# A finished expert's output copies moved into the code between experts

## The chip, the cores and the metric

One Trainium2 chip, one core of it. The metric is device time in microseconds (us) of one execution; the median of three runs of the kernel before is 878.82 us (875.96 to 879.72). Engines are named as in the profile: PE multiplies matrices (PEld loads its weights), ACT, DVE and POOL work on rows of data, SP issues DMAs. PSUM is the memory that PE writes to, SBUF the memory that the others work in.

## The reference, cut to what matters

Three stages follow one another. An attention stage with 4 batches, 8 heads, 512 local and 32 global tokens gives a matrix `x` of 2176 tokens by 512. A mixture of 8 experts then sends each token to one expert:

```python
logits = x @ w_gate
expert_idx = np.argmax(logits, axis=1)
for e in range(E):                      # 8 experts
    mask = expert_idx == e
    xe = x[mask]
    h = np.maximum(xe @ w1[e], 0.0)     # 512 -> 1024
    out[mask] = gate_w[mask, None] * (h @ w2[e])   # 1024 -> 512
```

A last feed-forward stage computes `(h - tanh(h)) @ w_out` with `h = x @ w_in` (512 to 2048 to 512). How many tokens an expert gets is known only while the kernel runs. Products are formed from a high and a low part of each operand, in three matmuls, to keep float32 accuracy.

## The kernel before

The attention stage scatters each token's row to its expert's list in DRAM (`xs`). The experts are then worked through in eight places, 0 to 7; which expert stands at which place is chosen by how many tokens each has. At a place the code is this:

- `put_ids` (L1228) copies the token numbers of the place's rows to `ids`.
- `place(e)` (L1195) is a tree of comparisons on the place's token count. It ends in one of several arms, written out one after the other in the program: one for each width from the place's largest down to 256 in steps of 32, and one for 128. Each engine compares and jumps for itself.
- Each arm is a whole expert at a fixed width N. `expert` (L1105) goes through eight blocks m of 128 hidden units: first layer into `pL1` (L1010), ReLU and split into high and low by ACT (L1013) and DVE (L1014), second layer into the four PSUM banks `pL2` (L1021), two blocks behind. `expert_small` (L1126) is the arm for 128 tokens, with operands exchanged; its result is in the bank `pL2[0]`, is added up in SBUF (L1181) and transposed by PE back into `pL2[0]` (L1183).
- Both arms end with the outputs: copies from PSUM to the tiles `yst` (`emit_Y`, L1026, two on ACT and two on DVE at width N; L1185 in the small arm, one on each) and four DMAs from `yst` to the output matrix `yc` in DRAM (L1027, L1192), at a column that is known only at run time.
- After the tree all arms meet again. `emit_XT` (L995) brings in the next place's rows: for each of four k, PE transposes the tiles of `xrow` into a PSUM bank (L999), ACT casts the bank into the high part `xT[0]` (L1001) and DVE subtracts it from the bank into the low part `xT[1]` (L1002). The banks are `pX[0]`, `pX[1]`, `pL1[1]` and again `pX[0]`, so that the fourth transposes wait for DVE's first subtraction. `load_x` (L987) then has SP fetch the rows of the place after next.

Beside this, all through the arms, the experts' weights arrive by DMA in `raw` buffers (L120, L122), six blocks ahead, and ACT, DVE and POOL split them into high and low (`split_from`, L928 to L937); in some blocks DVE and ACT also convert the last stage's weights (`conv_bits`, L942). Just before its outputs an arm splits two blocks of the next expert's weights (`ahead` and `split`).

`hint(e + 1)` (L1212) is a small tree of comparisons in each arm, after block 2 (after the first pair of blocks but one in the small arm). Its leaf marks the next place's arm, and puts a prefetch instruction for that branch on each engine. In the last place the branch marked is `over` (L1285), which is taken when an expert has more than 512 tokens.

The last arm of place 7 also starts the last stage: `split_y0`, and `emit_H(0)` (L1053) ahead of its own outputs.

The order is written out by hand; engines run their own queues in order and wait for each other by semaphores.

Of the kernel before, what the change touches and what calls it, by code (L numbers as in the profile page):

```python
# [46 lines left out]
def body(ctx: ExitStack, tc: tile.TileContext, q_l, k_l, v_l, q_g, k_g, v_g,  # L47
         w_gate, w1, w2, w_in, w_out, out):
    nc = tc.nc
# [7 lines left out]
    KD = DM // 128  # L57
# [10 lines left out]
    idf = const.tile([128, 128], F32, name="idf")  # L68
# [36 lines left out]
    yc = [dram.tile([128, T + CAP], F32, name=f"yc{k}") for k in range(KD)]  # L105
# [18 lines left out]
    def load_raw(c):  # L124
        if c < NC:
            load_w(raw[c % NR], eids[c // MF], c % MF)
# [57 lines left out]
    for kind in ("first", "mid", "last"):  # L184
        m = attc.tile([128, W], F32, name=f"mask_{kind}")
# [135 lines left out]
    for j in range(4):  # L321
# [6 lines left out]
                          in_=tokid[:, 0:NXB * NB])  # L328
# [392 lines left out]
    for n in range(lo, NT0):  # L721
# [4 lines left out]
        if n == lo:  # L726
# [8 lines left out]
            for j in range(B):  # L735
                nc.sync.dma_start(out=vg[:, j].rearrange("g (h d) -> g h d", h=H),
                                  in_=v_g[j].rearrange("h g d -> g h d"))
# [86 lines left out]
    for w in LAST.split():  # L824
        t, m = w.split(".")
# [88 lines left out]
    pX = [psL.tile([128, 512], F32, name=f"pX_{j}") for j in range(2)]  # L914
    pL2 = [psL.tile([128, 512], F32, name=f"pL2_{j}") for j in range(4)]
# [6 lines left out]
    yst = [mc.tile([128, 512], F32, name=f"yst{j}") for j in range(4)]  # L922

    def split(c, eng=None):
        if c < NC:
            split_from(raw[c % NR].bitcast(F32), c % NS, eng)
# [60 lines left out]
    def load_x(e, step=2):  # L987
        if e >= E:
            return
        v = xsr[bass.ds(xos[e], CAP), :].rearrange("(j p) w -> p j w", p=128)  # L990
        for j in range(0, tiles(e), step):
            r = slice(j, min(j + step, tiles(e)))
            nc.sync.dma_start(out=xrow[:, r], in_=v[:, r])
# [10 lines left out]
    def emit_L1(s, m, N, first=False):  # L1004
        ps = pL1[m % 2]

        for c in (slice(0, 256), slice(N - 256, N)) if first and N > 256 else (slice(0, N),):
            for a, x in ((0, 0), (1, 0), (0, 1)):
                for k in range(KD):
                    nc.tensor.matmul(ps[:, c], w1s[s][a][:, k], xT[x][:, k, c], start=a + x + k == 0,  # L1010
                                     stop=x == 1 and k == KD - 1)
        h = hT[m % 3]
        nc.scalar.activation(out=h[0][:, 0:N], in_=ps[:, 0:N], func=ACTF.Relu)  # L1013
        nc.vector.scalar_tensor_tensor(out=h[1][:, 0:N], in0=ps[:, 0:N], scalar=0.0, in1=h[0][:, 0:N].bitcast(F32),  # L1014
                                       op0=ALU.max, op1=ALU.subtract)

    def emit_L2(s, m, N):
        h = hT[m % 3]
        for j in range(KD):
            for a, x, st, sp in ((0, 0, m == 0, False), (0, 1, False, False), (1, 0, False, m == MF - 1)):  # L1020
                nc.tensor.matmul(pL2[j][:, 0:N], w2s[s][a][:, 128 * j:128 * (j + 1)], h[x][:, 0:N], start=st, stop=sp)  # L1021

    def emit_Y(N, yo):
        for j in range(KD):
            copy = nc.vector.tensor_copy if j % 2 else nc.scalar.copy
            copy(out=yst[j][:, 0:N], in_=pL2[j][:, 0:N])  # L1026
            nc.sync.dma_start(out=yc[j][:, bass.ds(yo, N)], in_=yst[j][:, 0:N])  # L1027
# [11 lines left out]
    while t0 < T:  # L1039
        n = min(NB2, T - t0)  # L1040
# [20 lines left out]
    def load_wout():  # L1061
        for m in range(PW, PW + NO):
            wout_load(m)
# [12 lines left out]
    def tiles(p):  # L1076
        return -(-sizes(p)[0] // 128)


    def sizes(p):  # L1080
        most = T // (RANKS[p - 1] + 1) if p else T
        most = min(CAP, 32 * -(-most // 32))
        return tuple(range(most, 255, -32)) + (128,)
# [18 lines left out]
        if (e, m) in convs:  # L1102
            pre_conv1(convs[e, m], tmp64)

    def expert(e, N, yo):  # L1105
        for m in range(MF):
            c = e * MF + m
            emit_L1(c % NS, m, N, c == 0)
            if m > 1:
                emit_L2((c - 2) % NS, m - 2, N)  # L1110
            ahead(e, m)
            if m == 2:
                hint(e + 1)
        split((e + 1) * MF + LS)
        load_raw((e + 1) * MF + LS + NR)
        if e == E - 1:
            split_y0()
            load_wout()
        for m in range(MF - 2, MF):
            emit_L2((e * MF + m) % NS, m, N)  # L1120
        if e == E - 1:
            emit_H(0)
        emit_Y(N, yo)


    def expert_small(e, yo):  # L1126
        NQ = MF // 2

        def L1(q, ks):
            s = (e * MF + 2 * q) % NS  # L1130
            ps = pL1[q % 2][:, 0:256]
            for k in ks:
                for a, x, st, sp in ((0, 0, k == 0, False), (0, 1, False, False), (1, 0, False, k == KD - 1)):
                    nc.tensor.matmul(ps, xT[x][:, k, 0:128], w1a[a][:, s:s + 2, k, :], start=st, stop=sp)
            if q > 0 and KD - 1 in ks:
                nc.scalar.activation(out=hs[q % 2], in_=ps, func=ACTF.Relu)
            elif len(ks) == KD:
                nc.vector.tensor_scalar(out=hs[q % 2], in0=ps, scalar1=0.0, scalar2=None, op0=ALU.max)

        def TH(q):  # L1140
            pt = pX[q % 2][:, 0:256]
            for i in range(2):
                nc.tensor.transpose(pt[:, 128 * i:128 * (i + 1)], hs[q % 2][:, 128 * i:128 * (i + 1)], idf)
            t = hT[q % 3]
            nc.scalar.copy(out=t[0][:, 0:256], in_=pt)
            nc.vector.tensor_tensor(out=t[1][:, 0:256], in0=pt, in1=t[0][:, 0:256].bitcast(F32), op=ALU.subtract)


        def L2(q, c=slice(0, DM), ps=pL2[0]):
            last = NQ - 1  # L1150
            for i in range(2):
                m = 2 * q + i
                s = (e * MF + m) % NS
                for a, x, st, sp in ((0, 0, q in (0, last) and i == 0, False), (0, 1, False, False),
                                     (1, 0, False, q in (last - 1, last) and i == 1)):
                    nc.tensor.matmul(ps[:, c], hT[q % 3][x][:, 128 * i:128 * (i + 1)], w2s[s][a][:, c],
                                     start=st, stop=sp)

        for q in range(NQ):
            first = (KD, 2, 1, 1)[q]  # L1160
            L1(q, range(first))
            if q > 0:
                TH(q - 1)
            if q or e == 0:
                split(e * MF + 2 * q + LS, nc.vector)
            L1(q, range(first, KD))
            if q > 0:
                L2(q - 1)
            ahead(e, 2 * q, None, True)
            if q < NQ - 1:  # L1170
                ahead(e, 2 * q + 1, nc.vector, True)
            if q == 1:
                hint(e + 1)
        if e == E - 1:
            split_y0()
            load_wout()
        TH(NQ - 1)
        nc.scalar.copy(out=yst[3], in_=pL2[0])
        for c, ps in ((slice(0, 256), pX[0]), (slice(256, 512), pL1[0])):
            L2(NQ - 1, c, ps)  # L1180
            nc.vector.tensor_tensor(out=yst[2][:, c], in0=ps[:, c], in1=yst[3][:, c], op=ALU.add)  # L1181
        for k in range(KD):
            nc.tensor.transpose(pL2[0][:, 128 * k:128 * (k + 1)], yst[2][:, 128 * k:128 * (k + 1)], idf)  # L1183
        for c, copy in ((slice(0, 256), nc.scalar.copy), (slice(256, 512), nc.vector.tensor_copy)):
            copy(out=yst[3][:, c], in_=pL2[0][:, c])  # L1185
        ahead(e, MF - 1, nc.vector, True)
        split((e + 1) * MF + LS)
        load_raw((e + 1) * MF + LS + NR)
        if e == E - 1:
            emit_H(0)  # L1190
        for k in range(KD):
            nc.sync.dma_start(out=yc[k][:, bass.ds(yo, 128)], in_=yst[3][:, 128 * k:128 * (k + 1)])  # L1192


    def place(e, i=0):  # L1195
# [8 lines left out]

    def arm(e, n):
        if n == 128:
            expert_small(e, yos[e])
        else:
            expert(e, n, yos[e])


    def hint(e, lo=0, hi=None):  # L1212
# [15 lines left out]
    def put_ids(xr, yo):  # L1228
        nc.sync.dma_start(out=ids[bass.ds(yo, CAP), :], in_=xsr[bass.ds(xr, CAP), DM:DM + 1])
# [10 lines left out]
    for c in range(LS):  # L1240
        split(c)
        if c + NR < MF:
            load_raw(c + NR)
    banks = pX + pL2
    cnts = values(0, 0, mybir.ALL_ENGINES, T)
    hint(0)
    for j in range(4):
# [10 lines left out]
    yos = values(2, 0, SP, T) + values(2, 1, SP, T)  # L1258
    cnts += values(0, 1, mybir.ALL_ENGINES, T)
    for e in range(E):  # L1260
        put_ids(xos[e], yos[e])
        if e == E - 1:
            mxc = nc.values_load(offi[0:1, 3, 0:1], min_val=0, max_val=T)
            with tc.If(mxc <= CAP):
                load_y0()
        place(e)
        if e + 1 < E:
            emit_XT(range(KD), (pX[0], pX[1], pL1[1], pX[0]), tiles(e + 1))
            load_x(e + 2)


    def block_over(e, xb, j, yo):
# [148 lines left out]
    for c in range(NCH + LO):  # L1421
# [10 lines left out]
        if wo_hl:  # L1432
            m = wo_hl.pop(0)
            conv_hl(tmpo[m % 2], wo[m][0], wo[m][1], nc.gpsimd)
        emit_v(c)
        if wo_next[0] < M2 and 4 * (c - WL) >= 5 * (wo_next[0] - PW):
            m = wo_next[0]
# [40 lines left out]
```

## Time and profile before

| | us |
|---|---|
| median of three runs (875.96 to 879.72) | 878.82 |
| the profiled execution | 877.86 |
| its span, first to last instruction | 876.1 |
| PE busy | 797.0 |
| DVE busy | 668.2 |
| ACT busy | 484.2 |
| POOL busy | 324.9 |

The mean granted clock of PE in that execution is 0.974 of full speed. The profile's page gives busy time by engine, the span in forty slices, the DMA queues, the chain of work that ended last, and the costliest groups of instructions. Behind it stand views of the same trace: the timeline (instructions in order of time), sums by stretches, the waits and the records of single lines. Times in them are microseconds from the start of the span. In this execution the places ran with widths 480, 512, 128, 320, 128, 288, 256 and 256; the experts take from 188 to 476 us, the last stage from there to the end.

### The profile page before, as it was taken

The page shows a single profiled execution, that of the slowest core. Times are in us where ns is not written, and L with a number is a line of the kernel's source. Part 1 is how long each engine was busy: PE and PEld are TensorE (multiplying, and loading weights), DVE is VectorE, ACT ScalarE, POOL GpSimd, SP SyncE. Part 2 cuts the span into 40 slices and gives each one's busy share as a digit, 9 for nine tenths or more (in the row PEclk, how much of TensorE's full clock was granted, in tenths as well). Part 3 has the DMA queues.
Part 4 walks back from the last instruction along what each step waited for, and adds up shares of the span by engine and source line. Part 5 has one row for each costly group of instructions (what it writes and reads, how often), then busy time and mean ns, then how long its engine had stood idle before and what let it go on. Part 6 is the DMA issues. An engine that isn't in the chain of part 4 may idle for free. (4 is left out here: it accounts for less than half of the span.)

```text
span 876.1 us, 16545 instructions
## 1 busy us (share of the span) xinstructions
PE 797.0 (91%) x5456; PEld 694.6 (79%) x5456; DVE 668.2 (76%) x1428; ACT 484.2 (55%) x1177; POOL 324.9 (37%) x405
## 2 busy tenths in 40 slices
PE   8989999969899787796969988999999999999997
PEld 6767777758788687686969866799899999998885
DVE  6879999854568676775546999988788778778784
ACT  6777877533334343353524655565565566556564
POOL 8222352423213334342511565533433333343332
PEclk9999999979999899998979999999999999999999
DMA  6699964445846798889533223010000010010000
GB/s 146 148 266 228 271 175 139 135 146 151 251 144 205 185 217 246 213 199 297 164 70 101 65 107 108 1 46 28 13 34 28 1 46 19 1 43 1 13 25 24
DMA packets 145261, 102.96 MB, mean 118 GB/s; under 512 B 76608, under 2 KB 124224, under 8 KB 145088
## 3 DMA queue, kind: packets, MB, share of 16 engines
q1 hardware_dynamic: 142368, 92.08, 39.0%
q0 software_dynamic: 2720, 8.95, 2.7%
q8 instruction: 63, 1.03, 0.5%
q14 instruction: 110, 0.90, 0.4%
HBM read 78.75 MB, written 22.27 MB: 115 GB/s over the span
## 5 line engine op out<-in xcount | busy, mean ns | idle before, releaser
L1371 POOL TENSOR_TENSOR u<-u,z 128x384 f32<-128x384 f32 (+1 forms) x96 | 122.1, 1271 | 226.3 <-ACT u L1369 226.2
L936 POOL TENSOR_TENSOR w2s<-raw,w2s 128x512 fp32r<-128x512 f32 x64 | 90.8, 1427 | 199.7 <-ACT w2s L935 155.2
L1010 PE MATMUL pL<-xT,w1a 128*128 128x256 f32 (+4 forms) x588 | 109.6, 344 | 20.1 <-issue 8.5
L1010 PEld LDWEIGHTS pL<-xT,w1a 128*128 128x128 f32 x588 | 96.6, 210 | 29.7 <-issue 12.1
L1399 PE MATMUL pL<-wo,gT 128*128 128x512 f32 x417 | 108.9, 394 | 0.0
L1021 PE MATMUL pL<-hT,w2s 128*128 128x256 f32 (+4 forms) x576 | 98.6, 324 | 0.0
L1021 PEld LDWEIGHTS pL<-hT,w2s 128*128 128x128 f32 x576 | 87.7, 190 | 6.5
L1399 PEld LDWEIGHTS pL<-wo,gT 128*128 128x128 f32 x417 | 77.5, 188 | 14.3
L1386 DVE TENSOR_TENSOR gT<-g,gT 128x384 fp32r<-128x384 f32 (+1 forms) x64 | 79.1, 1236 | 0.7 <-ACT gT L1364 0.7
L365 ACT ACTIVATE P<-sc,mx 128x224 f32<-128x224 f32 x128 | 60.6, 477 | 12.0 <-DVE mx L356 11.4
L1376 DVE TENSOR_TENSOR g<-pL,z 128x384 f32<-128x384 f32 (+1 forms) x64 | 34.0, 531 | 42.9 <-ACT d L1359 42.9
L1053 PE MATMUL pL<-xT,wih 128*128 128x384 f32 x256 | 65.2, 335 | 1.5 <-DVEq L1285 1.5
L936 DVE TENSOR_TENSOR w1a<-raw,w1a 128x512 fp32r<-128x512 f32 x64 | 62.9, 986 | 4.1 <-ACT w1a L935 2.9
L1358 ACT ACTIVATE z<-pL 128x384 f32<-128x384 f32 (+1 forms) x64 | 30.2, 472 | 62.9 <-PE pL L1053 59.4
L1014 DVE SCALAR_TENSOR_TENSOR hT<-pL,hT 128x256 fp32r<-128x256 f32 (+4 forms) x48 | 25.0, 520 | 50.1 <-ACT hT L1013 42.7
L1053 PE MATMUL pL<-yB,wih 128*128 128x384 f32 (+1 forms) x256 | 59.5, 318 | 0.0
L1369 ACT ACTIVATE u<-z,c1t 128x384 f32<-128x384 f32 (+1 forms) x96 | 58.2, 606 | 0.0
L1370 ACT ACTIVATE mk<-z,nth 128x384 bf16<-128x384 f32 (+1 forms) x96 | 56.8, 592 | 0.0
L1382 DVE SCALAR_TENSOR_TENSOR g<-u,g 128x384 f32<-128x384 f32 (+1 forms) x96 | 55.0, 573 | 0.0
L1399 PE MATMUL pL<-wo,xT 128*128 128x512 f32 x207 | 54.4, 395 | 0.0
L1013 ACT ACTIVATE hT<-pL 128x256 fp32r<-128x256 f32 (+4 forms) x48 | 22.2, 463 | 52.3 <-PE pL L1010 52.3
L1053 PEld LDWEIGHTS pL<-xT,wih 128*128 128x128 f32 x256 | 46.7, 188 | 4.3 <-ACTq L1285 1.8
(294 smaller groups left out, 1889.3 us busy)
## 6 DMA issues: line engine op xcount, KB each, us to landing
raw<-in_moe_w_dram SPq DMA_DIRECT2D x128, 256.0 KB, 5.1
xs<-zrow SPq DMA_DIRECT2D x32, 258.0 KB, 4.8
raw<-in_moe_w_in_dram SPq DMA_DIRECT2D x16, 512.0 KB, 5.0
raw<-in_moe_w_out_dram SPq DMA_DIRECT2D x16, 512.0 KB, 3.6
xrow<-xs SPq DMA_DIRECT2D x12, 516.0 KB, 5.1
nk<-in_k_l_dram SPq DMA_DIRECT2D x32, 128.0 KB, 3.6
nq<-in_q_l_dram SPq DMA_DIRECT2D x32, 128.0 KB, 3.7
v<-in_v_l_dram SPq DMA_DIRECT2D x12, 256.0 KB, 4.5
```

Source lines behind the costliest of these rows:

```text
L365: nc.scalar.activation(out=P[:, j, 0:W], in_=sc[:, j], func=ACTF.Exp, scale=-1.0, bias=mx[:, j:j + 1], accum_out=sums[n][:, 2 * ip + j, h: ...
L936: (nc.gpsimd if lo else nc.vector).tensor_tensor(out=dl, in0=t[:, lo:lo + 512], in1=dh.bitcast(F32), op=ALU.subtract)
L1010: nc.tensor.matmul(ps[:, c], w1s[s][a][:, k], xT[x][:, k, c], start=a + x + k == 0, stop=x == 1 and k == KD - 1)
L1021: nc.tensor.matmul(pL2[j][:, 0:N], w2s[s][a][:, 128 * j:128 * (j + 1)], h[x][:, 0:N], start=st, stop=sp)
L1053: nc.tensor.matmul(ps[:, 0:n], a[:, m, k], y[x][:, k, 0:n], start=st, stop=sp)
L1369: nc.scalar.activation(out=u, in_=z, func=ACTF.Identity, scale=C2, bias=c1t)
L1370: nc.scalar.activation(out=mk, in_=z, func=ACTF.Relu, bias=nth)
L1371: nc.gpsimd.tensor_tensor(out=u, in0=u, in1=z, op=ALU.mult)
L1376: nc.vector.tensor_tensor(out=g, in0=h, in1=z, op=ALU.mult)
L1382: nc.vector.scalar_tensor_tensor(out=g, in0=u, scalar=C0, in1=g, op0=ALU.add, op1=ALU.mult)
L1386: nc.vector.tensor_tensor(out=t[1][:, 0:n], in0=g, in1=t[0][:, 0:n].bitcast(F32), op=ALU.subtract)
L1399: nc.tensor.matmul(p, g[a][:, 128 * j:128 * (j + 1)], w, start=st, stop=sp)
```

## The change

The copies and the output DMAs leave the arms. `emit_Y` is called once for each place, in the common code after the tree: behind `emit_XT` and `load_x`, so after the casts of the next place's rows. Its width is no longer the arm's N but the largest of the place: 512 at places 0, 1, 3, 5 and 7, 320 at place 2, 384 at place 4, 448 at place 6. The small arm's transposes write to the first 128 columns of four banks, so that `emit_Y` finds its outputs where it finds those of the other arms; its own two copies and four DMAs go. The first place's rows are transposed into `pL2` in place of `pX` and two banks of `pL2`. `hint` moves from block 2 to block 0 (in the small arm from the second pair to the first).

```diff
-    def expert(e, N, yo):
+    def expert(e, N):
...
             ahead(e, m)
-            if m == 2:
+            if m == 0:
                 hint(e + 1)
...
         if e == E - 1:
             emit_H(0)
-        emit_Y(N, yo)
-    def expert_small(e, yo):
+    def expert_small(e):
...
-            if q == 1:
+            if q == 0:
                 hint(e + 1)
...
         for k in range(KD):
-            nc.tensor.transpose(pL2[0][:, 128 * k:128 * (k + 1)], yst[2][:, 128 * k:128 * (k + 1)], idf)
-        for c, copy in ((slice(0, 256), nc.scalar.copy), (slice(256, 512), nc.vector.tensor_copy)):
-            copy(out=yst[3][:, c], in_=pL2[0][:, c])
+            nc.tensor.transpose(pL2[k][:, 0:128], yst[2][:, 128 * k:128 * (k + 1)], idf)
         ahead(e, MF - 1, nc.vector, True)
         split((e + 1) * MF + LS)
         load_raw((e + 1) * MF + LS + NR)
         if e == E - 1:
             emit_H(0)
-        for k in range(KD):
-            nc.sync.dma_start(out=yc[k][:, bass.ds(yo, 128)], in_=yst[3][:, 128 * k:128 * (k + 1)])
...
-    banks = pX + pL2
+    banks = pL2
...
         if e + 1 < E:
             emit_XT(range(KD), (pX[0], pX[1], pL1[1], pX[0]), tiles(e + 1))
             load_x(e + 2)
+
+        emit_Y(sizes(e)[0], yos[e])
```

## Rows read from the trace of the kernel before

**Rows 1.** Sums by stretch: length, busy time (count) per engine, clock, DMA share, GB/s.

```profile
181.00:478.00 297.00, 249.67 (x1478) 223.94 (x1479) 182.80 (x269) 120.47 (x246) 90.34 (x64) 0.93 0.68 189
478.00:862.00 384.00, 373.66 (x1923) 333.69 (x1922) 324.07 (x522) 232.01 (x520) 161.68 (x142) 1.00 0.10 33
```

**Rows 2.** Timeline, places 0 to 1: start, length, instruction, [idle before <-what ended it].

```profile
228.79 0.62 ACT L935 CAST w2s<-raw 128x512 fp32r<-128x512 f32 x1 [0.24 <-issue]
...
233.52 0.56 ACT L1026 COPY yst<-pL 128x480 f32<-128x480 f32 x1 [0.74 <-PE pL L1021]
...
234.76 1.10 PE L999 MATMUL pX<-idf,xrow 128*128 128x128 f32 x8 [0.62 <-issue]
...
236.20 1.07 ACT L1001 CAST xT<-pX 128x512 fp32r<-128x512 f32 x2 [2.12 <-PE pX L999]
...
237.63 1.29 DVE L1002 TENSOR_TENSOR xT<-pX,xT 128x512 fp32r<-128x512 f32 x2 [2.80 <-ACT xT L1001]
...
239.91 10.06 PE L1010 MATMUL pL<-xT,w1a 128*128 128x512 f32 x36 [0.81 <-ACT xT L1001]
```

**Rows 3.** Timeline, places 1 to 2.

```profile
282.49 0.62 ACT L935 CAST w2s<-raw 128x512 fp32r<-128x512 f32 x1
...
284.69 0.59 ACT L1026 COPY yst<-pL 128x512 f32<-128x512 f32 x1 [0.77 <-PE pL L1021]
...
285.70 0.85 PE L999 MATMUL pX<-idf,xrow 128*128 128x128 f32 x6 [0.37 <-issue]
...
289.38 0.86 ACT L1001 CAST xT<-pX 128x384 fp32r<-128x384 f32 x2 [4.10 <-issue]
...
290.60 1.02 DVE L1002 TENSOR_TENSOR xT<-pX,xT 128x384 fp32r<-128x384 f32 x2 [4.54 <-ACT xT L1001]
...
291.83 3.92 PE L1134 MATMUL pL<-w1a,xT 128*128 128x256 f32 x18
```

**Rows 4.** PE's jump records near 281 and 352 us: count, min/median/max ns, start.

```profile
L1200 PEldq COMPARE_BRANCH  x1: 4418/4418/4418, 281.1 to 281.1; - x1
...
L1200 PEldq COMPARE_BRANCH  x1: 2410/2410/2410, 351.9 to 351.9; - x1
```

**Rows 5.** Timeline, places 3 to 4.

```profile
350.23 0.88 PE L999 MATMUL pX<-idf,xrow 128*128 128x128 f32 x6 [1.46 <-issue]
...
354.58 2.38 PE L1134 MATMUL pL<-w1a,xT 128*128 128x256 f32 x18 [2.10 <-ACT w1a L935]
```

**Rows 6.** Sums by stretch around two boundaries; columns as in the first group.

```profile
240.70:244.10 3.40, 3.40 (x9) 2.63 (x8) 0.00 (x0) 0.00 (x0) 0.00 (x0) 0.50 0.61 183
244.10:250.00 5.90, 5.90 (x27) 4.88 (x26) 3.80 (x6) 2.23 (x4) 1.01 (x1) 1.00 0.01 1
348.00:355.00 7.00, 2.94 (x21) 2.23 (x20) 3.32 (x7) 2.77 (x6) 1.51 (x1) 1.00 0.87 277
```

**Rows 7.** Timeline, places 2 to 3, the small arm's end.

```profile
309.40 0.42 DVE L1181 TENSOR_TENSOR yst<-pL,yst 128x256 f32<-128x256 f32 x1 [0.23 <-PE pL L1156]
...
311.28 0.69 DVE L936 TENSOR_TENSOR w1a<-raw,w1a 128x512 fp32r<-128x512 f32 x1
```

**Rows 8.** Sums by stretch in place 3; columns as in the first group.

```profile
316.00:336.00 20.00, 16.32 (x112) 16.05 (x110) 11.33 (x17) 7.34 (x15) 5.58 (x4) 1.00 0.92 194
```

**Rows 9.** Timeline, place 3, PE's longest stop there and DVE ahead of it.

```profile
334.95 0.43 DVE L946 TENSOR_SCALAR tmp<-raw 128x512 int32<-128x512 int32 x1 [5.94 <-DMA raw<-in_moe_w_in_dram]
...
336.56 3.42 PE L1010 MATMUL pL<-xT,w1a 128*128 128x320 f32 x12 [4.24 <-DVE hT L1014]
```

**Rows 10.** PE's prefetch record in place 7, and the timeline behind it.

```profile
L1473 PEldq BRANCH_PREFETCH_HINT  x1: 41/41/41, 442.3 to 442.3; - x1
...
442.39 3.63 PE L1010 MATMUL pL<-xT,w1a 128*128 128x256 f32 x17 [3.74 <-issue]
450.60 4.42 PE L1010 MATMUL pL<-xT,w1a 128*128 128x256 f32 x19 [4.57 <-issue]
```

**Rows 11.** Waits of PE for nothing visible: us in total, times, longest.

```profile
PE pL L1010 <- issue: 8.5, 3, 4.6
```

More of the change, by code (lines that the diff above doesn't have):

```diff
@@ L1206, in arm @@
         if n == 128:
-            expert_small(e, yos[e])
+            expert_small(e)
         else:
-            expert(e, n, yos[e])
+            expert(e, n)
     def hint(e, lo=0, hi=None):
```

## The prediction

> **What bounds the kernel now.** Read the sums by stretch first [rows 1]. From 478 us on PE is busy 373.7 of 384 us, so whatever the experts save before that reaches the end. Between 181 and 478 us PE is busy 249.7 of 297 us at a granted clock of 0.93: some 47 us of idle time, and part of the busy time at the lower clock. The change acts on the boundaries between places, so the timeline there comes next.
>
> At places 0 to 1 [rows 2] ACT's last cast in the arm is at 228.79; it then waits for PE to finish the second layer, since its copies come last. The second copy starts at 233.52, and only behind it does ACT leave the arm. PE starts the next rows' transposes at 234.76, but ACT's first cast comes at 236.20 and DVE's first subtraction at 237.63, 0.84 us after that cast's result (two casts take 1.07, pipelined). DVE's subtraction lets PE make the fourth transposes, and the first layer starts at 239.91. At places 1 to 2 [rows 3] it is plainer: ACT's copy starts at 284.69, PE transposes at 285.70, and ACT's cast starts at 289.38 after 4.10 us idle "by issue", that is, waiting for nothing that the profile shows. The copies run up to the jump out of the arm, and from the jump to the common code ACT starts nothing for 2.7 us (233.52 to 236.20) and 4.7 us (284.69 to 289.38). [...]
>
> PE pays too, but earlier: its sequencer runs ahead of the array and jumps at 281.1 for 4.42 us [rows 4], while queued matmuls are still running, so only 0.37 us of idle time is left at 285.70 [rows 3].
>
> **The change part by part.** *Copies out of the arms, places 0 to 1.* The last work of ACT in the arm becomes the cast at 228.79, of DVE a subtraction at about the same time. ACT jumps 4.7 us sooner (233.52 less 228.79), more than the 2.7 us that the jump costs, and DVE likewise; both stand in the common code when PE's transposes arrive. Four transposes of the eight at 234.76 take about 0.6 us with their drain, so ACT's cast starts near 235.4, is done near 236.0, and DVE starts at 236.0 where it started at 237.63: 1.6 us. PE's fourth transposes, ACT's fourth cast and the first layer follow DVE at unchanged distances. Gain 1.6. What is late next is PE's walk through the comparisons, which sits inside the 0.81 us before 239.91 and moves with it.
>
> *Places 1 to 2.* ACT's jump moves from 284.7 to 282.5 [rows 3], so its 4.7 us end near 287.2 instead of 289.38: 2.2 us. But another wait takes over. At places 3 to 4 nothing of ACT is late, and still PE starts the small arm only at 354.58, because its jump into the arm at 351.9 takes 2.41 us [rows 4, 5]; that is 354.35, or 4.1 us after it entered the common code at 350.23. If the same 4.1 us hold from 285.70, PE can't start before 289.8, with the first matmul near 290.1, against 291.83. Gain 1.7; without that bound 2.2 to 3.0.
>
> *The clock.* [...] In place 2 the first 18 matmuls take 3.92 us [rows 3] against 2.38 us for the same 18 in place 4 [rows 5]: 1.54 us. At places 3 to 4 PE was busy only 2.94 of 7.00 us and the clock stayed at 1.00 [rows 6]. With the stops cut by 1.6 and 1.7 us I count both falls as gone: 3.0 us; the bounds are 0 and 3.0.
>
> *The small arm, places 2 to 3 and 4 to 5 (one pattern, two times).* DVE's last sum ends at 309.82 and its next useful work starts at 311.28 [rows 7]; between lie the copies L1185, which wait for ACT's copy and PE's transposes. They go, so DVE starts up to 1.46 us earlier, and the first layer of the next place follows DVE. I take 1.4 each, 2.8 together; bounds 0 and 2.9.
>
> *Boundaries 3 to 4, 5 to 6, 6 to 7 and the end of place 7.* PE's own jump is the last to arrive, as the 1.46 us "by issue" at 350.23 show [rows 5]. Nothing is gained; I take 0.
>
> *The copies in their new place.* Two on ACT and two on DVE, at up to 512 columns 0.59 us each on ACT [rows 3], a little more on DVE: 1.2 and 1.4 us, behind the casts. PE is then in the first layer, 36 matmuls in 10.06 us [rows 2], and ACT is next needed when the first twelve are done; the bank `pL2` is not written before that. So cost 0. If that cover were gone, each boundary would pay up to 1.4 us.
>
> *The wider writes.* On SP the four output DMAs now stand behind `load_x` and ahead of `put_ids` and the next weight loads. `load_x` no longer waits for them. Their bytes grow with the fixed width: places 2 and 4 from 128 columns to 320 and 384, which is 0.39 and 0.52 MB more (columns x 512 B x 4). These two are followed by places with conversions: in place 3 the DMA share is 0.92 at 194 GB/s [rows 8], and DVE stops 5.94 us for a weight load and PE behind it 4.24 us [rows 9]. At 194 GB/s the extra bytes are 2.0 and 2.7 us, the upper end if each delays the loads behind it in full: 4.7. The lower end is 0: the engines have 8% left, and SP, one issue behind another, reaches `load_x` sooner. I take 2.2, near the middle. At places 1, 3, 5 and 6 the write grows by 0 to 0.46 MB too, but nothing there stops PE for a load.
>
> [...]
>
> *The hint.* It moves ahead by two blocks. It adds no instruction. I take 0; the rivals hold both ends.
>
> **Sum.** 1.6 + 1.7 + 3.0 + 2.8 = 9.1 us saved, less 2.2 for the writes: 6.9. The profiled execution took 877.86 us (span 876.1 and 1.8 around it), which gives 871.0; the median of the runs is 1 us above the profiled one. I say 871.5.
>
> **The rivals.** *The saving is taken up by what is late next.* At 1 to 2 PE's jump ends even later than 290.1, the clock still falls, and the writes cost their full 4.7: 1.6 + 1.0 + 2.8 - 4.7 leaves about 1 us, 877.5. For it: DVE and PE already stop for loads in place 3 [rows 9]. Against it: at 0 to 1 nothing else is near.
>
> *The early hint starves PE (the slower side).* In place 7 the prefetch record stands at 442.3, at the arm's start [rows 10]; PE issues 17 matmuls and then stops 4.57 us by issue, as if the next stretch of its own code had not been fetched. Elsewhere the hint came after block 2, when PE's queue was full, and no such stop is seen: the three stops by issue ahead of L1010 sum to 8.5 us [rows 11], of which 4.57 and 3.74 are place 7's. At block 0 the queue is shorter. The price is up to 4.57 us at each of places 1 to 6. Two such stops cancel the forecast gain; from three (13.7 us) the kernel is slower: 871.5 + 13.7 = 885.2. [...]
>
> [...]
>
> *The early hint helps PE.* PE's jumps into the arms of places 4, 6 and 7 cost it 2.4 us [rows 4] to 3.74 us [rows 10]. If the earlier mark has them fetched in time, some 7 us more go: 864.5.
>
> *The change doesn't do what it says:* the casts still wait, for instance since a wait at the meeting of the arms covers all of DVE's work. Then the time is 878.
>
> **How the numbers follow.** Forecast 0.50 (866 to 876), taken up 0.20, hint starves 0.13, hint helps 0.14, no effect 0.03. The range 863.5 to 881 leaves out about 2 in 10, mostly the slow end. A measurement of this kernel tells about 0.5% from no change, 4.4 us here, so faster means below 874.4: most of the forecast (0.42) and hint helps (0.14), together 0.56. Within 0.5%: the rest of the forecast, taken up, no effect, and a hint that stops PE twice, 0.33. Slower: 0.11.
>
> **What would show it.** In the changed kernel's timeline ACT's first cast at 0 to 1 and 1 to 2 follows PE's first transposes by under 1.5 us; the copies L1026 start behind the casts, under the first layer; the clock stays at 1.00 through the start of places 1 and 2; L1185 is gone and DVE goes from L1181 straight to L936. The forecast is wrong if PE stops by issue inside the first blocks of a place, if PE's stop in place 3 grows by more than 2 us, or if the first layer of place 2 still starts 6 us after PE's first transpose.

## The result, and the profile after

Timed side by side, the changed kernel takes 869.88 us (median of five, 866.97 to 871.08) and the kernel before 877.89 (875.96 to 879.72): a ratio of 0.990, 95% interval 0.987 to 0.993. The profiled execution of the changed kernel took 869.88 us, with a span of 868.2, against 871.5 forecast. In a second comparison (below) it took 866.26, ratio 0.986 (0.981 to 0.991).

The sums by stretch of the kernel after; columns: stretch, length, busy time (count) of PE, PEld, DVE, ACT and POOL, granted clock, DMA share, GB/s.

```profile
181.00:470.00 289.00, 251.25 (x1477) 225.23 (x1478) 185.33 (x272) 122.90 (x250) 90.39 (x64) 0.93 0.72 203
470.00:862.00 392.00, 382.07 (x1956) 339.79 (x1956) 328.81 (x532) 235.39 (x529) 163.32 (x145) 1.00 0.11 33
```

The experts end near 470 us where they ended near 478, and PE idles there for 37.8 us in place of 47.3. The clock is 0.93 as it was [rows 1].

The timeline of the kernel after at places 0 to 1 (start, length, instruction, idle before and what ended it):

```profile
227.99 0.62 ACT L935 CAST w2s<-raw 128x512 fp32r<-128x512 f32 x1 [0.24 <-issue]
...
233.74 1.10 PE L999 MATMUL pX<-idf,xrow 128*128 128x128 f32 x8 [0.41 <-issue]
234.44 1.07 ACT L1001 CAST xT<-pX 128x512 fp32r<-128x512 f32 x2 [5.82 <-PE pX L999]
...
235.06 1.29 DVE L1002 TENSOR_TENSOR xT<-pX,xT 128x512 fp32r<-128x512 f32 x2 [5.87 <-ACT xT L1001]
...
235.80 0.55 PE L999 MATMUL pX<-idf,xrow 128*128 128x128 f32 x3 [0.53 <-DVE xT L1002]
...
237.63 0.37 PE L999 MATMUL pX<-idf,xrow 128*128 128x128 f32 x1 [1.28 <-issue]
...
238.52 1.08 ACT L1026 COPY yst<-pL 128x512 f32<-128x512 f32 x2
...
238.77 2.49 PE L1010 MATMUL pL<-xT,w1a 128*128 128x512 f32 x5 [0.77 <-ACT xT L1001]
239.26 1.28 DVE L1026 COPY yst<-pL 128x512 f32<-128x512 f32 x2
```

ACT's cast follows the first transposes by 0.70 us and DVE's subtraction starts as the cast ends. (The prediction's sign, a cast within 1.5 us, told nothing at this boundary: it was 1.44 before [rows 2].) PE's wait for that subtraction, ahead of the fourth transposes, is 0.53 us; in the kernel before it was 2.08:

```profile
238.38 0.73 PE L999 MATMUL pX<-idf,xrow 128*128 128x128 f32 x4 [2.08 <-DVE xT L1002]
```

The copies stand behind the casts, beside the first layer. But of the fourth transposes three come at once and the last 1.28 us later, with PE waiting for nothing visible.

Places 1 to 2 in the kernel after, with the record of PE's jump into the small arm (count, min/median/max ns, start) below it:

```profile
285.43 0.88 PE L999 MATMUL pX<-idf,xrow 128*128 128x128 f32 x6
286.01 0.86 ACT L1001 CAST xT<-pX 128x384 fp32r<-128x384 f32 x2 [2.93 <-PE pX L999]
...
287.04 1.02 DVE L1002 TENSOR_TENSOR xT<-pX,xT 128x384 fp32r<-128x384 f32 x2 [3.68 <-ACT xT L1001]
...
290.76 1.62 PE L1133 MATMUL pL<-w1a,xT 128*128 128x256 f32 x6 [2.56 <-ACT w1a L935]
```

```profile
L1195 PEldq COMPARE_BRANCH  x1: 2948/2948/2948, 287.7 to 287.7; - x1
```

ACT starts its cast at 286.01 where it started at 289.38 [rows 3]. That it leaves the arm earlier stands in the records of its own jumps (kernel before, then after; the first of the two after is the one out of the arm):

```profile
L1200 ACTq COMPARE_BRANCH  x1: 68/68/68, 284.7 to 284.7; - x1
```

```profile
L1195 ACTq COMPARE_BRANCH  x2: 65/66/68, 281.5 to 288.3; - x2
```

PE's jump into the small arm ends at 290.6, and the first layer follows at 290.76: the bound that the prediction named, 0.7 us later than it said. (The view names ACT as the releaser; PE's sequencer arrived last.)

The clock around these boundaries, the small arm's end, PE's stop in place 3, and place 7, all in the kernel after:

```profile
237.70:244.60 6.90, 6.13 (x15) 4.65 (x16) 1.88 (x3) 1.82 (x4) 0.00 (x0) 0.51 0.78 268
289.00:295.80 6.80, 5.04 (x23) 5.07 (x24) 2.86 (x6) 1.66 (x5) 0.60 (x1) 0.50 0.86 273
316.00:336.00 20.00, 16.30 (x105) 16.04 (x105) 11.93 (x19) 7.71 (x17) 5.59 (x4) 0.93 0.68 207
```

```profile
308.39 0.42 DVE L1180 TENSOR_TENSOR yst<-pL,yst 128x256 f32<-128x256 f32 x1 [0.23 <-PE pL L1155]
...
308.74 0.68 DVE L936 TENSOR_TENSOR w1a<-raw,w1a 128x512 fp32r<-128x512 f32 x1
```

```profile
333.91 3.31 PE L1010 MATMUL pL<-xT,w1a 128*128 128x320 f32 x12 [3.69 <-DVE hT L1014]
```

```profile
439.95 7.21 PE L1010 MATMUL pL<-xT,w1a 128*128 128x256 f32 x36 [3.89 <-issue]
```

The clock still falls at both boundaries, to 0.51 and 0.50; at 0 to 1 for longer than before [rows 6]. DVE goes from its last sum to the next weights with 0.35 us between the starts, 1.88 before [rows 7]. In place 3 the DMA share is 0.68 (0.92 before [rows 8]) and the stop 3.69 us (4.24 before [rows 9]): the wider writes did not lengthen it in this pair. In place 7 PE runs 36 matmuls in a row; the stop of 4.57 us after the 17th [rows 10] is gone. From its last matmul in place 6 to the last stage, the two kernels differ by 4.8 us, more than at any boundary. No step of the prediction said so, and the experiments begin there.

### The profile page after: what moved, and what is told of

Its sections match the earlier page's. It is cut to its first block, busy times and chain, and to the rows that moved or that the text cites. A ratio compares the mean times of both kernels' runs of the same rounds, so it can differ in the third digit from the quotient of the medians.

```text
span 868.2 us, 16570 instructions
## 1 busy us (share of the span) xinstructions
PE 801.0 (92%) x5456; PEld 698.1 (80%) x5456; DVE 670.7 (77%) x1430; ACT 485.5 (56%) x1179; POOL 324.5 (37%) x405
## 5 line engine op out<-in xcount | busy, mean ns | idle before, releaser
L1361 ACT CAST gT<-g 128x384 fp32r<-128x384 f32 (+1 forms) x64 | 31.8, 496 | 31.8 <-DVE g L1387 31.8
```

## The experiments

The theories: A, the saving comes from the copies that left the arms; B, the hint's place decides where PE stops by issue, place 7's stop among them; C, the early hint starves PE. Beside them, that PE's stops depend on where its code lies: the change takes one instruction out of PE's code, at the end of the arms of place 1, so all behind it lies one earlier (counted in the compiled code).

**The hint alone, and the move alone.** In the kernel before:

```diff
-            if m == 2:
+            if m == 0:
                 hint(e + 1)
...
-            if q == 1:
+            if q == 0:
                 hint(e + 1)
```

> The kernel before with the hint alone moved to the first block; the copies stay in the arms. Theory A (the saving comes from the copies that left the arms, the hint's place is worth nothing): 877.9, the same as before, DVE still waits for the copies at places 0 to 1, 1 to 2 and 2 to 3, and PE still stops 4.57 us inside place 7. Theory B (the hint's place decides where PE stops for its own code): 872 to 873.5, since place 7's stop of 4.57 us goes and the boundaries stay as they were. Theory C (the early hint starves PE): stops of 2 to 5 us by issue in the first blocks of places 1 to 6, 883 or more.

876.48 us, ratio 0.997 (0.994 to 1.000). The stop in place 7 is still there, after the same 17 matmuls:

```profile
441.74 3.79 PE L1010 MATMUL pL<-xT,w1a 128*128 128x256 f32 x17 [3.53 <-issue]
449.13 3.13 PE L1010 MATMUL pL<-xT,w1a 128*128 128x256 f32 x13 [3.59 <-issue]
```

The reverse of this diff in the changed kernel leaves only the move of the copies:

> The changed kernel with the hint back behind the third block; only the copies are moved. Theory A: 870, the first layer of place 3 still starts 1.4 us sooner after the transposes than before, and place 7 has no stop. Theory B: 874 to 875, with a stop of some 4.6 us in place 7 and the boundaries of the changed kernel.

866.20 us, ratio 0.985 (0.981 to 0.990), boundary 2 to 3 at 2.66 us, no stop in place 7. So B and C fall, and A holds: the move gives the whole saving, by whatever way the stop in place 7 goes with it. The hint is worth 0 to 0.6% alone, and with the copies out nothing that shows (0.985 with the late one, 0.990 and 0.986 with the early one, each uncertain by 0.003 to 0.005). In place 6 PE stops 0.79 and 0.80 us by issue in the two profiles of the changed kernel, behind 12 matmuls, and 0.60 in one other kernel with the early hint; in the four others with the early hint it does not, nor in any with the late one.

**Place 7's mark left out of the kernel before.**

```diff
-            tc.mark_branch_hint_location("over", engines=list(mybir.ALL_ENGINES))
```

> The kernel before without the mark for the code behind place 7, which stands at the start of the arm of place 7. If the marked code takes the room of PE's next stretch: the 4.57 us stop in place 7 is gone, and the time is 873 to 874, less up to 4 us that the jump behind place 7 may cost in its stead. If the stop is an accident of where the code lies or of when it is fetched, it stays, and the time is 878.

878.94 us, ratio 1.000 (0.997 to 1.004). The stop stays (3.15 us), so it does not hang on the mark. But it comes after 21 matmuls, not 17:

```profile
444.11 3.96 PE L1010 MATMUL pL<-xT,w1a 128*128 128x256 f32 x21 [3.31 <-issue]
451.23 2.08 PE L1010 MATMUL pL<-xT,w1a 128*128 128x256 f32 x12 [3.15 <-issue]
```

The marks' absence puts this arm 9 instructions earlier, and counted in the compiled code both stops come before instruction 31138. The jump behind place 7 now costs 5.41 us; with the mark it costs 3.02 in the kernel before and 2.11 to 3.77 in all thirteen profiles that have it (records of the kernel before, then of this one):

```profile
L1285 PEldq COMPARE_BRANCH  x1: 3017/3017/3017, 473.6 to 473.6; - x1
```

```profile
L1284 PEldq COMPARE_BRANCH  x1: 5410/5410/5410, 472.9 to 472.9; - x1
```

**Code moved, work unchanged.** Both kernels with matmuls added to an arm of place 0 that is not taken:

```diff
             emit_L1(c % NS, m, N, c == 0)
+            if e == 0 and m == 0 and N == 512:
+                for _ in range(5):
+                    emit_L2(c % NS, m, 128)
```

> The kernel before with 60 more second-layer matmuls in an arm of place 0 that is not taken; nothing more is executed, but all the code behind that arm lies 120 of PE's instructions further on. If PE's stops depend on where the code lies: the 4.57 us stop in place 7 goes or stands elsewhere, stops by issue in the common code move by 1 to 4 us, and the time changes by 2 to 6 us in either direction. If only the order of the work decides: 877.9, with the same stop in place 7 and the same boundaries to 0.3 us.

> The changed kernel with the same 60 matmuls in the arm that is not taken, so all code behind lies 120 instructions further on, as in the shifted kernel before (879.0). If the moved copies save 3 to 4 us at any layout and the rest was layout: 873 to 876, boundaries 0 to 1 and 1 to 2 together 1.4 us shorter and 2 to 3 and 4 to 5 each 1.4 us shorter than in the shifted kernel before, which had jumps of 2.9 to 3.2 us there. If the saving is all the copies' and layout is an accident that evens out: 870 to 871.

Before, shifted: 879.04, ratio 1.000 (0.996 to 1.003), the same time by other stops. Boundary 6 to 7 is 3.40 us (6.23 unshifted) and arm 7 24.35 (31.71), but boundaries 2 to 3, 3 to 4 and 4 to 5 grow by 2.7, 6.4 and 3.1. After, shifted: 869.84, ratio 0.991 (0.988 to 0.994). Boundaries 0 to 1 and 1 to 2 fall by 1.7 and 2.5 against the shifted kernel before; 2 to 3 does not shrink but grows by 3.0, to 9.78, since a jump of 6.75 us stands there:

```profile
L1198 PEldq COMPARE_BRANCH  x4: 68/76/6752, 305.3 to 305.7; - x4
```

**Only the code from place 6 on moved.** The same edit with `e == 6 and N == sizes(6)[0]`:

> The kernel before with 60 second-layer matmuls in an arm of place 6 that is not taken: places 0 to 5 keep their code where it was, the common code of places 6 to 7 and place 7 lie some 126 of PE's instructions further on. No executed work changes. If the code's position decides PE's stops: place 7's stop of 3 to 4.6 us goes and the jump into place 7 (3.0 us) goes too, as in the kernel shifted from place 0 on (boundary 3.40, arm 7 24.35), while the boundaries 2 to 3, 3 to 4 and 4 to 5 stay at 4.1, 5.8 and 3.9: 868 to 871, so that a shift of code alone buys as much as the change. If not: 877 to 879.

> The changed kernel with the same shift from place 6 on. If position decides: boundary 6 to 7 goes from 6.2 to 3.4 and arm 7 from 26.7 to 25.7, the rest as in the changed kernel: 862 to 863.5 where the changed kernel took 866.3. If not: 866 to 868. It is the candidate for the best version.

Before: 868.94, ratio 0.991 (0.988 to 0.994). A shift of code buys as much as the change. The jump into place 7, 3.06 us before, is 0.44 at most, and PE does not stop behind it (record, then timeline, of the shifted kernel before):

```profile
L1203 PEldq COMPARE_BRANCH  x2: 90/266/441, 438.1 to 438.2; - x2
```

```profile
438.82 4.57 PE L1010 MATMUL pL<-xT,w1a 128*128 128x256 f32 x36 [1.01 <-ACT xT L1001]
443.23 1.60 PE L1021 MATMUL pL<-hT,w2s 128*128 128x256 f32 x12
```

The 36 matmuls take 4.57 us, against 7.21 in the changed kernel, where the clock was at 0.50 after a stop of 3.89. After, shifted from place 6: 861.58, ratio 0.982 (0.978 to 0.985), boundary 6 to 7 at 3.39. That is the fastest version.

**Place 7's taken arm alone moved**, by 32 instructions, with `e == 7 and N == sizes(7)[0]` and `range(1)`:

> The kernel before with 12 matmuls in the largest arm of place 7, which is not taken: the arm of 256 columns that is taken starts 32 of PE's instructions further on, all else stays. Counted in the compiled code, the kernel before stopped at position 31138 after 17 matmuls, and the kernel without the mark, whose arm starts 9 earlier, at the same position after 21. If the stop belongs to that position: PE now stops after its first matmul of the arm, and until 8 us after it. If it belongs to the 18th matmul or to the moment: after 17 matmuls again, or not at all.

> The changed kernel with the same 12 matmuls in place 7's largest arm. If the stop in place 7 went because the code lies one instruction earlier, or by any other luck of position, it can come back: arm 7 at 29 to 34 in place of 26.7. If it went because the copies left the arms (ACT and DVE no longer jump beside PE), it stays away: arm 7 at 26 to 27, whatever the kernel before does with the same shift.

Before: 871.39, ratio 0.995 (0.991 to 0.999), no stop in place 7. After: 865.51 (two runs), ratio 0.986 (0.981 to 0.991), none either. So the fixed position by itself is refuted: this arm runs through instruction 31138 without a stop:

```profile
441.87 6.04 PE L1010 MATMUL pL<-xT,w1a 128*128 128x256 f32 x36 [4.03 <-issue]
```

**The writes' width.** The changed kernel with `emit_Y((480, 512, 128, 320, 128, 288, 256, 256)[e], yos[e])`, alone and with the late hint, and beside them the changed kernel as it is:

> The changed kernel with each place's copies at the width that its arm takes for these inputs (480, 512, 128, 320, 128, 288, 256, 256), which is right for these inputs alone: 2.75 MB less is written. If the wider writes delay the loads behind them (the prediction's term of 2.2 us, 0 to 4.7): 865 to 868 beside 870 for the changed kernel, with PE's stop in place 3 down from 3.69 to under 2 us. If they cost nothing: 870, and that stop stays at 3.5 to 4.2.

> The changed kernel once more, on the same chip as the others of this call: 870, ratio 0.990. Its profile says which stops stay from run to run: the 1.28 us of PE at places 0 to 1, no stop in place 7 and the 2.29 us at places 4 to 5 if the code's place decides them; others if they are chance.

> Only the move, with the hint behind the third block and the widths of these inputs. If the late hint is the better one once the copies are out (866.2 alone) and the narrow writes give something too: 862 to 866. If the late hint's 866.2 was chance: the same as the changed kernel with these widths, to 1.5 us. It is the candidate for the best version.

867.06, 866.26 and 864.99: ratios 0.984 (0.979 to 0.990), 0.986 (0.981 to 0.991) and 0.984 (0.979 to 0.990). The 2.75 MB less buy nothing that can be told from zero, but intervals of this width could not tell 2.2 us from zero either. PE's stop in place 3 says more: it is 3.30, 3.14 and 4.90 us; the kernel with the late hint and wide writes has 4.10, those shifted from place 6 and in place 7 have 2.37 and 4.53, and with the copies in the arms it is 1.28 to 4.24. Its size does not follow the width.

## Why the prediction was right, and where its sum was not

The stretch from the last matmul of a place's arm (at 2 to 3 and 4 to 5 the last transpose of its outputs) to the first of the next first layer, worked out from the timelines. The means are over the profiles in which the code up to place 6 lies as in the two kernels, five with the copies in the arms and seven without (6 to 7: without the two shifted from place 6 on, four and six); ranges in brackets.

| boundary | predicted | copies in the arms, us | copies out, us | difference |
|---|---|---|---|---|
| 0 to 1 | -1.6 | 5.70 (5.23 to 5.91) | 4.92 (4.52 to 5.44) | -0.8 |
| 1 to 2 | -1.7 | 6.15 (5.93 to 6.50) | 5.48 (4.92 to 5.97) | -0.7 |
| 2 to 3 | -1.4 | 4.07 (4.06 to 4.10) | 2.68 (2.65 to 2.80) | -1.4 |
| 3 to 4 | 0 | 6.74 (5.81 to 8.05) | 5.74 (4.90 to 6.48) | -1.0 |
| 4 to 5 | -1.4 | 3.94 (3.93 to 3.97) | 3.02 (2.52 to 4.28) | -0.9 |
| 5 to 6 | 0 | 7.01 (6.21 to 8.06) | 6.64 (6.22 to 7.09) | -0.4 |
| 6 to 7 | 0 | 6.15 (5.80 to 6.52) | 6.17 (6.01 to 6.38) | 0.0 |

*Right.* The mechanism: ACT and DVE jump while PE still multiplies, and the casts follow the transposes (at 1 to 2 in the kernel after ACT's jump is at 281.5 and DVE's at 282.6, PE's second layer ends at 285.3, and the first cast starts 0.58 us after the first transposes). At 0 to 1 PE's wait for DVE's first subtraction is 1.74 to 2.72 us in the five profiles with the copies in the arms and 0.53 in all seven without: the 1.6 that was counted. The small arm at 2 to 3 gave 1.4 to the tenth. And the saving does not hang on place 7: at three other positions of the code, where neither kernel stops there, the ratio is 0.991, each time against the kernel before with the same shift (0.9819/0.9909, 0.9909/0.9995, 0.9860/0.9948, each uncertain by some 0.005 to 0.007). That is 8 us, with 4 to 6 either way. In these three pairs of profiles the boundaries fall by 3.6, 3.5 and 6.4 us together; the rest is not placed. (With all code moved, 4.7 of the 10.2 us between the two spans lie in arm 0, which differs by up to 3.8 us between profiles with the copies in.)

The four boundaries for which a gain was forecast give 3.8 us where 6.1 were counted. Another 1.4 came at 3 to 4 and 5 to 6, where 0 was taken, with ranges that overlap. There PE's jump into the arm got shorter on average (at 3 to 4 it takes 2.29 to 3.92 us with the copies in and 1.54 to 2.70 with them out); no run shows why.

*The copies in their new place* cost nothing that shows: they lie beside the first layer, and the arms of places 0 to 6 together take 212.1 us with the copies in (210.3 to 213.4) and 212.3 with them out (210.0 to 216.1), in the same twelve profiles. The exception is place 7 in the changed kernel with all code, or that from place 6 on, moved. There SP issues a load of the last stage's weights 13.3 and 13.9 us into the arm, against 7.9 and 8.0 in the kernels before with the same shifts. DVE waits for it, PE behind DVE, and arm 7 is 1.4 and 1.9 us longer. SP now has the output DMAs ahead of it; whether they make it late, no run shows. In the changed kernel shifted from place 6 on:

```profile
452.15 0.43 DVE L946 TENSOR_SCALAR tmp<-raw 128x512 int32<-128x512 int32 x1 [2.94 <-DMA raw<-in_moe_w_out_dram]
453.70 1.69 PE L1010 MATMUL pL<-xT,w1a 128*128 128x256 f32 x12 [1.89 <-DVE hT L1014]
```

*"PE's fourth transposes, ACT's fourth cast and the first layer follow DVE at unchanged distances"* (0 to 1) failed, and with it *"what is late next is PE's walk through the comparisons"*. What is late next is PE's own issue. In all seven profiles it stops between the third and the last of the fourth transposes, 0.28 to 1.28 us, and takes back about half of the 1.6; in the one with all code shifted it does not, and there the boundary gained 1.7.

*The bound at 1 to 2* was the right one and was set too early: PE's jump into the small arm took 2.30 to 3.52 us in six of the seven profiles (1.54 in one), against the 2.41 taken over from another boundary [rows 4]. What the prediction did not see is that this jump cost nothing before: in the five profiles with the copies in the arms it takes 0.44 to 0.46 us. PE came to it some 5 us after its first transposes; now it comes 2.2 to 3.4 us after them, and stands in it instead of waiting for DVE. So most of what ACT and DVE gave up there, PE's jump took.

*"I count both falls as gone"* (3.0 us: 1.54 from the 18 matmuls of places 2 and 4 [rows 3, 5], and 1.43 from nine matmuls that took 3.40 us at a clock of 0.50, where the 27 behind them took 5.90 at 1.00 [rows 6]) failed. At 1 to 2 the clock still fell in all seven profiles, at 0 to 1 in five. The stops got shorter by 0.7 us, and PE still idled. The one quiet example, 3 to 4 [rows 6], did not carry over: with the copies in the arms the clock fell there in two profiles of five, and at 0 to 1 in three of five. So no gain of the clock shows, and whether it falls changes from profile to profile.

*4 to 5* gave the full 1.4 in three profiles of seven. In the other four the next wait is a weight load, on which ACT's casts ahead of the rows' stand: in the first profile of the changed kernel ACT waits 1.07 and 1.19 us for `raw`, its cast of the rows starts at 371.61, 2.4 us after the first transpose, and PE stops 2.29 us:

```profile
370.36 0.62 ACT L935 CAST w1a<-raw 128x512 fp32r<-128x512 f32 x1 [1.19 <-DMA raw<-in_moe_w_dram]
...
371.61 1.06 ACT L1001 CAST xT<-pX 128x512 fp32r<-128x512 f32 x2
...
372.96 0.66 PE L999 MATMUL pX<-idf,xrow 128*128 128x128 f32 x4 [2.29 <-DVE xT L1002]
```

*The wider writes* (2.2 us) were probably mis-sized: nothing of them shows in the stop in place 3 or in the arms, which speaks for the lower bound, 0; the times alone can't tell.

*The rivals.* Of *taken up by what is late next* two parts came (PE's late jump at 1 to 2, the clock), not the third, the writes. *The hint* at 0 was right to what can be measured, and neither of its rivals happened at the size that was feared or hoped for: of the stops inside the first blocks, the prediction's own sign of being wrong, one came, the 0.79 us in place 6. The stop in place 7, taken there as the hint's work, was not: it stays with the mark left out.

*Not foreseen:* place 7. The stop of 3.2 to 4.6 us is in three of three profiles with the arm's code as in the kernel before (with the mark, or without it and 9 instructions earlier), and in none of the eleven others. In the first pair of profiles it is 5.0 us of the 7.9 by which the spans differ (arm 7: 31.71 to 26.73), on average 4.2 (30.5 to 26.3, without the kernels shifted from place 0 or 6 on). So that 871.5 lies near 869.88 is in part luck. Of the 6.9 forecast, the clock's 3.0 and 2.3 at the four boundaries did not come; the 2.2 for the writes was not seen to be paid; and 1.4 at the other boundaries and some 4 in place 7 came, which nothing in it held.

*Open:* why it stops there. What PE does in such a stop, or in a jump of 3 us, no run shows; that its code had not been fetched was the author's supposition. The stop came before one instruction in two layouts, after 17 and after 21 matmuls, but an arm that begins two instructions ahead of that point passed it. Whether the change removed the stop because the code lies one instruction earlier or because ACT and DVE no longer jump at the same time stays open, since at the other positions neither kernel has it.

## What to carry to other kernels

Work that ends an arm should leave it when the engine can jump earlier. Here ACT jumped at 281.5 in place of 284.7 at 1 to 2, under PE's work, and the gain was 0.7 us on average, since PE's own jump then set the boundary. That jump took 0.44 to 0.46 us while PE came to it late, and 1.54 to 3.52 us once the wait was gone. Before a gain of 1% is credited to an edit of a program with large arms, both versions should be timed at a second position of the code: here added code that never runs was as strong an edit (0.991 from place 6 on), or did nothing (1.000 from place 0 on). And the clock that fell after the stop at 1 to 2 did not come back when the stop got 0.7 us shorter.

## What the hardware showed beside that

At one jump of PE a prefetch mark seems to be worth some 2 us: 2.11 to 3.77 us in thirteen profiles with it, 5.41 in the one without. PE's jump into place 7, over the same work, took about 3 or under 0.5 us by the position of the code alone, and another (2 to 3) 0.35 or 2.9 to 6.8. One kernel, profiled two times, differs by up to 1.8 us in a single stretch and by 4.2 in its span: sums of one profile against one other can't carry terms below 2 us.
